# A two-layer attention and MLP kernel: one write and one read for each LayerNorm tile that is transposed through DRAM, Q and K weights loaded by halves, and a new written-out order

## The chip, the cores and the metric

The kernel runs on one core of a Trainium2 chip. A core has TensorE (PE, matrix multiplication), VectorE (DVE), ScalarE (ACT), GpSimd (POOL) and SyncE (SP), which here only issues DMAs, and 16 DMA engines that move data between the on-chip memory and DRAM. The metric is the device time of one execution in microseconds (us), lower is better. Three timed executions of the kernel before took 459.1, 463.7 and 463.11 us, so the median is 463.11 us.

## What is computed

The input x has 2048 rows of 512 features, in bf16. Two layers follow each other, each an attention and an MLP, with the same weights both times:

```python
x = x + attention(layernorm(x))
x = x + mlp(layernorm(x))
x = x + attention(layernorm(x))
x = x + mlp(layernorm(x))

# attention: 32 heads of 16, a query sees its own key and the 255 before it
qkv = x @ wqkv                                  # 512 -> 3 * 512
p = softmax(where(mask, q @ k.T * 16 ** -0.5, -1e9))
return (p @ v) @ wo
# mlp
return gelu(x @ w1 + b1) @ w2 + b2              # 512 -> 1792 -> 512
# layernorm
(x - mean) / sqrt(var + 1e-5)
```

## The kernel before

**Tiles.** The 2048 rows are 16 tiles of 128 rows; since there are two layers, the code counts 32 tiles `tau`, 0 to 31, where tile 16 is tile 0 in the second layer. Attention goes in 16 blocks `b` of two tiles. For each block the code makes Q (`lnq`), K and V (`kv`), then in `attention` the scores (`visit`: matmuls of 32 by 64, and an exponential on ScalarE, L938), the mask (L959, on VectorE or POOL), the product with V (`pv`), the output projection and the residual sum into X (`outproj`, `residual`). The MLP runs in ten jobs `J` of two or four tiles (`mlp`): W1, gelu on ScalarE, W2, residual sum. A block of attention needs the Q of the next block too, as a key is seen by the 255 queries behind it.

**LayerNorm and the transposition.** `layernorm(tau, layer, ...)` (L726) serves both: `layer` 0 is the one ahead of attention, `layer` 1 the one ahead of the MLP. Statistics are taken on VectorE (L733, L735), eps is added on VectorE (L737), POOL takes the power -0.5 (L740), and VectorE scales the tile into `xn` (L743). A matmul wants the features on the partitions, so the tile must be transposed. It goes one of two ways. Early tiles, and the last two ahead of the MLP, go through TensorE (L769 to L778) and are copied to `xnTA` (attention) or `xnTB` (MLP). The others, for which `by_dma` is true (tiles 4 to 29 ahead of the MLP, 14 to 31 ahead of attention, 44 in all), go through DRAM: VectorE transposes blocks of 32 by 32 into `xs_` (L752), four DMAs of 32 partitions each write `xs_` to a scratch tensor in DRAM (L764), and one DMA reads it back in the transposed layout (L767). Ahead of attention the four writes are cut into runs of 64 bytes (2048 in a tile), ahead of the MLP into runs of 256 bytes (512 in a tile); the read is 128 rows of 1 KB in both. All five are issued by SP, in its order, and the read waits for all four writes.

**The loads.** `load` and `load_x` (L689, L694) issue the inputs at the start. SP's queue has X 0, X 2-3, X 4-7, b1, Wo, X 8-15, W1, W2, b2; ScalarE's queue has X 1 and then Wqkv in three parts of 512 columns: Q, K, V (L701 to L704). Here X n is tile n of x.

**What sets the order.** Every operation is added to a list by `add()` with its engine, the names that it reads and writes, and a duration that a planner once used. Some operations have an alternative engine (`alt`). Three tables are written out by hand: `ORDER`, the sequence in which the operations are issued (each engine runs its own in that sequence), `TURNS`, which of the alternatives is taken, and `BANKS`, which banks of PSUM each matmul group gets. `_List.run` goes through them and `_Sched.op` adds the semaphore waits. DMAs take 12 semaphores in turn, and a DMA waits for the one 12 places ahead of it. An engine never passes over a waiting instruction, so where an operation stands in `ORDER` decides what waits behind it. A read of a name waits for its last write: the names `Wqkv0`, `Wqkv1` and `Wqkv2` are the three parts of Wqkv, `xa..` the tiles of `xnTA`, `xb..` those of `xnTB`, `scr..` the places in DRAM.

## Time and profile before

| | before |
|---|---|
| timed executions | 459.1, 463.7, 463.11 us (median 463.11) |
| profiled execution | 460.17 us, its span 458.4 us, mean granted clock 0.996 |
| matmuls | 8690 records, 427.1 us busy |
| DMA | 22.88 MB, 68606 packets, 54188 of them under 512 bytes |
| issues of `xs_` to DRAM | 176, each 32 KB |
| reads back | 26 into `xnTB`, 18 into `xnTA`, each 128 KB |

How to read it: the span is the stretch of the profiled execution in which the core's engines worked; the execution's own time is 1.8 us more. "Busy" is the time in which an engine had an instruction in work, and "idle before" a group of instructions is put down to what released it: `<-DMA xnTB<-scr_x` is a wait for the transfer from the scratch tensor to `xnTB`. "SPq" and "ACTq" are the instruction queues of SP and ScalarE that issue DMAs. "PEld" is TensorE's weight load, beside the matmuls. The granted clock is the share of TensorE's full clock that it was given. A window's row has its start and end, its length, then for each engine busy us and (x instructions).

### The profile page before, as it was taken

How to read it: one execution, taken by the hardware profiler on the slowest of the kernel's cores; microseconds unless marked ns; L12 is line 12 of the kernel's file. 1: busy time of each engine (PE TensorE's matmuls, PEld its weight loads, DVE VectorE, ACT ScalarE, POOL GpSimd, SP SyncE). 2: the span in 40 equal slices, each digit the busy share in tenths (PEclk: the TensorE clock that was granted, in tenths of full speed). 3: DMA queues.
4: the chain of work that ended last, by engine and by line, in shares of the span. 5: the costliest groups of instructions: out<-in, count | busy, mean ns of one | idle time of the engine just before them, and what ended most of it. 6: DMA issues, size and time to landing. Idle time of an engine off the chain costs nothing.

```text
span 458.4 us, 19424 instructions
## 1 busy us (share of the span) xinstructions
PE 427.1 (93%) x8690; PEld 232.9 (51%) x8764; DVE 370.1 (81%) x753; ACT 388.6 (85%) x463; POOL 232.3 (51%) x266
## 2 busy tenths in 40 slices
PE   5998999988999999699999999999998899999997
PEld 2655564655444555354444535445463453445665
DVE  4899988899998999678998789999796868576432
ACT  2699999999999989689998999989998799884343
POOL 4277555564764645643657557364444532554120
PEclk9899999999999999999999999999999999999999
DMA  8910000001230232301132112302223012102011
GB/s 280 370 53 3 4 3 3 3 4 28 42 68 14 30 64 43 69 10 37 27 72 46 20 34 50 72 17 31 47 57 69 4 36 48 49 4 70 13 47 57
DMA packets 68606, 22.88 MB, mean 50 GB/s; under 512 B 54188, under 2 KB 68012, under 8 KB 68524
## 3 DMA queue, kind: packets, MB, share of 16 engines
q1 hardware_dynamic: 66796, 19.94, 19.7%
q10 hardware_dynamic: 1728, 1.70, 1.1%
q8 instruction: 68, 1.11, 1.0%
q14 instruction: 14, 0.11, 0.1%
HBM read 13.77 MB, written 7.86 MB: 47 GB/s over the span
## 4 chain that ended last, share of the span: by engine, by line
PE 60%; ACT 17%; DMA 8%; DVE 8%; SPq 4%; issue 3%; ACTq 0%; DVEq 0%
PE ps L32 59%; ACT E L938 12%; DMA scr_x<-xs_ 3%; SPq L764 3%; DMA xnTB<-scr_x 3%; ACT gT L1104 2%; DMA Wqkv_sb<-in_A_wqkv_dram 2%; DVE X L796 1%; ACT gT L1096 1%; DVE xs_ L752 1%; DVE E L959 1%; DVE stat L733 1%; DVE TT L1024 1%; DVE KT L859 1%; DVE QT L719 1%
## 5 line engine op out<-in xcount | busy, mean ns | idle before, releaser
L938 ACT ACTIVATE E<-ps 128x1024 bf16<-128x1024 f32 x304 | 286.4, 1046 | 27.1 <-PE ps L32 26.0
L959 POOL TENSOR_TENSOR E<-E,mask 128x512 bf16<-128x512 bf16 (+1 forms) x131 | 135.3, 1047 | 108.6 <-ACT E L938 41.4
L32 PE MATMUL ps<-xnTB,W_sb 128*128 128x512 bf16 (+1 forms) x560 | 115.6, 337 | 5.3 <-DMA xnTB<-scr_x 4.6
L32 PE MATMUL ps<-W_sb,gT 128*128 128x512 bf16 (+1 forms) x421 | 108.5, 373 | 5.4 <-issue 3.5
L32 PE MATMUL ps<-xnTA,Wqkv_sb 128*128 128x256 bf16 (+1 forms) x544 | 74.4, 271 | 5.5 <-DMA Wqkv_sb<-in_A_wqkv_dram 3.1
L32 PEld LDWEIGHTS ps<-xnTB,W_sb 128*128 128x128 bf16 x560 | 51.0, 98 | 50.1 <-DMA xnTB<-scr_x 4.9
L1104 ACT ACTIVATE gT<-ps,b1T 128x512 bf16<-128x512 f32 (+1 forms) x92 | 49.0, 590 | 23.8 <-PE ps L32 23.7
L32 PE MATMUL ps<-QT,KT 32*64 32x320 bf16 (+4 forms) x2976 | 65.2, 258 | 2.8 <-ACT E L938 2.0
L796 DVE TENSOR_TENSOR X<-X,ps 128x512 bf16<-128x512 bf16 x63 | 42.5, 679 | 27.4 <-PE ps L32 27.3
L32 PEld LDWEIGHTS ps<-W_sb,gT 128*128 128x128 bf16 x462 | 41.4, 98 | 42.7 <-issue 5.6
L32 PEld LDWEIGHTS ps<-xnTA,Wqkv_sb 128*128 128x128 bf16 x544 | 48.0, 100 | 27.2 <-ACT E L938 4.3
L740 POOL TENSOR_TENSOR rstd<-veps,mhalf 128x1 f32<-128x1 f32 x64 | 37.2, 588 | 40.1 <-DVE veps L737 39.5
L959 DVE TENSOR_TENSOR E<-E,mask 128x512 bf16<-128x512 bf16 (+1 forms) x131 | 49.5, 403 | 6.3 <-ACT E L938 6.3
L32 PEld LDWEIGHTS ps<-QT,KT 32*64 32x64 bf16 x2976 | 27.5, 103 | 49.9 <-ACT E L938 32.9
L1068 POOL TENSOR_TENSOR X<-X,b2b 128x512 bf16<-128x512 bf16 x32 | 36.8, 1156 | 31.5 <-DVE TM L1029 15.1
L1024 DVE STREAM_TRANSPOSE TT<-ps 128x1024 f32<-128x1024 f32 x32 | 39.9, 1248 | 13.4 <-PE ps L32 13.1
L32 PE MATMUL ps<-E,Va 64*17 64x128 bf16 (+3 forms) x3872 | 46.1, 229 | 4.5 <-issue 0.9
L32 PEld LDWEIGHTS ps<-E,Va 64*17 64x17 bf16 x3872 | 36.8, 85 | 20.0 <-PE ps L32 7.2
L733 DVE BATCH_NORM_STATS2 stat<-X 128x6 f32<-128x512 bf16 x64 | 43.4, 681 | 2.8 <-DMA X<-in_A_x_dram 2.1
L1093 DVE TENSOR_SCALAR gT<-ps,b1T 128x512 bf16<-128x512 f32 (+1 forms) x48 | 31.7, 671 | 12.2 <-PE ps L32 11.6
L859 DVE TENSOR_TENSOR KT<-ps,parmask 128x1024 bf16<-128x1024 f32 x30 | 36.2, 1213 | 4.9 <-PE ps L32 4.7
L1029 POOL TENSOR_TENSOR TM<-TT,Rc 128x512 bf16<-128x512 f32 x21 | 22.3, 1061 | 28.8 <-DVE Rc L1027 19.7
(51 smaller groups left out, 333.7 us busy)
## 6 DMA issues: line engine op xcount, KB each, us to landing
scr_x<-xs_ SPq DMA_DIRECT2D x176, 32.0 KB, 2.2
W_sb<-in_B_w_dram SPq DMA_DIRECT2D x2, 1792.0 KB, 17.8
xnTB<-scr_x SPq DMA_DIRECT2D x26, 128.0 KB, 2.3
xnTA<-scr_x SPq DMA_DIRECT2D x18, 128.0 KB, 2.4
out_dram<-X SPq DMA_DIRECT2D x15, 128.0 KB, 1.8
Wqkv_sb<-in_A_wqkv_dram ACTq DMA_DIRECT2D x3, 512.0 KB, 9.3
X<-in_A_x_dram SPq DMA_DIRECT2D x1, 1024.0 KB, 13.0
X<-in_A_x_dram SPq DMA_DIRECT2D x1, 512.0 KB, 7.7
```

What stands on the lines that cost most here:

```text
L32: return self.e.matmul(*a, **k)
L733: add("dve", lambda e, B: e.bn_stats(stat6[:, k6, :], X[:, t, :]), 590, reads=["X%d" % t], writes=["st%d" % k6], prio=prio)
L740: add("pool", lambda e, B: e.tensor_tensor(out=rstd[:, k : k + 1], in0=veps[:, k : k + 1], in1=mhalf[:], op=ALU.pow), 535, reads=["ve%d" % ...
L796: add("dve", lambda e, B: e.tensor_tensor(out=X[:, t, :], in0=X[:, t, :], in1=ps[:, B[g][0], :], op=ALU.add), d_psum(512), reads=["X%d" % ...
L859: add("dve", lambda e, B, g=g, i=i: e.tensor_tensor(out=KT[:, kb, :, 2 * i : 2 * i + 2, :].rearrange("p a c q -> p a (c q)"), in0=ps[:, B[ ...
L938: add("act", lambda e, B, g_=g_, gi=gi: e.activation(E[:, 2 * gi : 2 * gi + 2, e0 : e0 + 512], ps[:, B[g_][0] : B[g_][0] + 2, :], AF.Exp, ...
L959: op = lambda e, B, Ew=Ew, Mw=Mw: e.tensor_tensor(out=Ew, in0=Ew, in1=Mw, op=ALU.mult)
L1024: add("dve", lambda e, B: e.transpose(TT[:, s].rearrange("p a c q d -> p a (c q d)"), ps[:, B[g][0] : B[g][0] + 2, :].rearrange("p a n -> ...
L1029: mul = lambda e, B: e.tensor_tensor(out=TM[:, sm].rearrange("p c q a d -> p a (c q) d"), in0=TT[:, s, :, :, :, 0:Dh].rearrange("p a c q d ...
L1068: add("pool", lambda e, B: e.tensor_tensor(out=X[:, t, :], in0=X[:, t, :], in1=b2b[:], op=ALU.add), 1110, reads=["X%d" % t, "b2b"], writes ...
L1093: add("dve", lambda e, B, g=g, fc=fc: e.tensor_scalar(out=gT[:, fc, 0:M], in0=ps[:, B[g][0], 0:M], scalar1=b1T[:, fc : fc + 1], scalar2=No ...
L1104: add("act", lambda e, B, g=g, fc=fc: e.activation(gT[:, fc, 0:M], ps[:, B[g][0], 0:M], AF.Gelu_apprx_tanh, bias=b1T[:, fc : fc + 1], scal ...
```

## The change

Four things change.

1. The transposition through DRAM has one write in place of four. To allow it the features are permuted in one way for both layers (`(d j q)` where the MLP's had `(d q j)`), and the pieces of the layout that the four writes made are now made by the read. Ahead of the MLP the write is 128 rows of 1 KB and the read 512 runs of 256 bytes; ahead of attention the write is 512 runs of 256 bytes and the read 2048 runs of 64 bytes. The planned durations are new, with 0.7 us added from tile 12 on (`room`).
2. The columns of Q and of K in Wqkv are loaded as halves of 256 columns, in the order Q first half, K first half, Q second, K second, then V whole. They stand on SP's queue behind X 0. X 2-3 goes to ScalarE's queue behind X 1. The projections wait for the half that they use.
3. The addition of eps may run on POOL instead of VectorE.
4. `ORDER`, `TURNS` and `BANKS` are new throughout.

```diff
-        load_x(0, 1, 2600.0)
-        load_x(1, 1, 2700.0, "act")
-        for which, lands in enumerate((5000.0, 7000.0, 9800.0)):
-            load(lambda e, B, which=which: e.dma_start(
-                Wqkv_sb[:, :, which * D : (which + 1) * D],
-                A_wqkv[:, which * D : (which + 1) * D].rearrange("(c p) n -> p c n", p=P)), ["Wqkv%d" % which], lands, "act")
-        load_x(2, 2, 4700.0)
-        load_x(4, 4, 9000.0)
...
+        def load_w(lo, n, name, lands):
+            load(lambda e, B: e.dma_start(
+                Wqkv_sb[:, :, lo : lo + n], A_wqkv[:, lo : lo + n].rearrange("(c p) n -> p c n", p=P)), [name], lands)
+
+        load_x(0, 1, 2450.0)
+        load_x(1, 1, 2650.0, "act")
+        load_x(2, 2, 4500.0, "act")
+        for i, lands in enumerate((4600.0, 5500.0, 6300.0, 7200.0)):
+            load_w(i % 2 * D + i // 2 * D // 2, D // 2, "Wqkv%d_%d" % (i % 2, i // 2), lands)
+        load_w(2 * D, D, "Wqkv2", 9000.0)
+        load_x(4, 4, 10700.0)
...
-            add("dve", lambda e, B: e.tensor_scalar(
-                out=veps[:, k : k + 1], in0=statmv[:, k, 1:2], scalar1=EPS, scalar2=None, op0=ALU.add), 75,
-                reads=["mv%d" % k], writes=["ve%d" % k], prio=prio - 300)
+            eps = lambda e, B: e.tensor_scalar(
+                out=veps[:, k : k + 1], in0=statmv[:, k, 1:2], scalar1=EPS, scalar2=None, op0=ALU.add)
+            add("dve", eps, 75, reads=["mv%d" % k], writes=["ve%d" % k], prio=prio - 300, alt=(("pool", eps, 130),))
...
+                order_ = "p (q d j) -> p d q j" if layer else "p (d q j) -> p d q j"
                 add("dve", lambda e, B: e.transpose(
-                    xs_[:, z, :].rearrange("p (q d j) -> p d q j", q=4, d=DC), 
-                    xn[:, s, :].rearrange("p (d q j) -> p d q j" if layer else "p (d j q) -> p d q j", q=4, d=DC)), 630,
+                    xs_[:, z, :].rearrange(order_, q=4, d=DC), xn[:, s, :].rearrange("p (d j q) -> p d q j", q=4, d=DC)), 630,
                     reads=["xn%d" % s], writes=["xs%d" % z], prio=prio)
                 flat = scr[v].rearrange("p c -> (p c)")
-                for r in range(4):
-                    if layer:
-                        to = scr[v].rearrange("(q j) (r c) -> r j q c", j=32, r=4)[r]
-                        src = xs_[32 * r : 32 * r + 32, z, :].rearrange("j (q c) -> j q c", q=4)
-                    else:
-                        to = flat.rearrange("(j x r k) -> r j x k", j=32, r=4, k=32)[r]
-                        src = xs_[32 * r : 32 * r + 32, z, :].rearrange("j (x k) -> j x k", k=32)
-                    dma(lambda e, B, to=to, src=src: e.dma_start(to, src), ["scr%d_%d" % (v, r)], reads=["xs%d" % z],
-                        prio=prio, dur=2000.0 if layer else 3000.0, issue=400.0)
-                to = dst.rearrange("p r d j -> p (r d j)") if layer else xnTA[:, tau // 2 % 2, tau % 2].rearrange("p c t -> p (c t)")
-                dma(lambda e, B, to=to: e.dma_start(to, scr[v]), [dname], reads=["scr%d_%d" % (v, r) for r in range(4)], prio=prio, dur=2300.0, issue=420.0)
+                if layer:
+                    put = lambda e, B: e.dma_start(scr[v], xs_[:, z, :])
+                    get = lambda e, B: e.dma_start(
+                        dst.rearrange("p r d j -> p r (d j)"), flat.rearrange("(r p c) -> p r c", r=4, p=P))
+                else:
+                    put = lambda e, B: e.dma_start(
+                        flat.rearrange("(d p c) -> p d c", d=DC, p=P), xs_[:, z, :].rearrange("p (d c) -> p d c", d=DC))
+                    get = lambda e, B: e.dma_start(
+                        xnTA[:, tau // 2 % 2, tau % 2].rearrange("p d (r k) -> p (d r) k", r=4),
+                        flat.rearrange("(x p k) -> p x k", x=16, p=P))
+                room = 0.0 if tau < 12 else 700.0
+                dma(put, ["scr%d_0" % v], reads=["xs%d" % z], prio=prio, dur=(2200.0 if layer else 2500.0) + room, issue=440.0 if layer else 600.0)
+                dma(get, [dname], reads=["scr%d_0" % v], prio=prio, dur=(2700.0 if layer else 3600.0) + room, issue=600.0 if layer else 1100.0)
                 return
...
-                         P, DC, ["xa0_%d" % j, "Wqkv%d" % which], prio, fresh=(j == 0))
+                         P, DC, ["xa0_%d" % j, "Wqkv%d_%d" % (which, kc // 2)], prio, fresh=(j == 0))
...
-                         256, 2, xr + ["Wqkv%d" % which], prio, fresh=(half == 0), war=war)
+                         256, 2, xr + ["Wqkv%d_%d" % (which, i)], prio, fresh=(half == 0), war=war)
```

## The prediction

> **What bounds the kernel now.** I read the page's busy times first, then the waits of TensorE, then its busy time by windows, and last the chain and the timeline of the two places where TensorE stands still.

> ```profile
> span 458.4 us, 19424 instructions
> PE 427.1 (93%) x8690; PEld 232.9 (51%) x8764; DVE 370.1 (81%) x753; ACT 388.6 (85%) x463; POOL 232.3 (51%) x266
> ```

> ```profile
> PE ps L32 <- issue: 7.2, 40, 0.9
> PE ps L32 <- DMA xnTB<-scr_x: 5.7, 4, 3.3
> PE ps L32 <- ACT E L938: 4.8, 17, 0.5
> PE ps L32 <- DMA Wqkv_sb<-in_A_wqkv_dram: 3.1, 2, 2.0
> ```

> ```profile
> 0.00:5.00 5.00, 3.76 (x9) 1.34 (x10) 1.92 (x6) 1.28 (x1) 3.66 (x17) 1.00 0.60 187
> 5.00:11.00 6.00, 2.68 (x25) 1.57 (x23) 3.40 (x13) 1.19 (x2) 1.75 (x3) 1.00 1.08 352
> 11.00:15.00 4.00, 3.93 (x44) 3.75 (x45) 2.14 (x4) 1.53 (x4) 0.00 (x0) 0.65 1.10 360
> ...
> 20.00:30.00 10.00, 9.87 (x175) 5.63 (x183) 9.76 (x24) 10.00 (x13) 7.75 (x8) 1.00 0.50 160
> ...
> 190.00:200.00 10.00, 8.44 (x200) 4.65 (x201) 5.46 (x12) 6.11 (x7) 4.17 (x7) 1.00 0.41 71
> ...
> 340.00:350.00 10.00, 8.42 (x244) 4.20 (x253) 7.04 (x13) 8.03 (x9) 7.51 (x7) 1.00 0.37 56
> ```

> The second fence is us in total, times, longest. The columns of the third are PE, PEld, DVE, ACT and POOL busy, granted clock, DMA share, GB/s. TensorE works 427.1 of 458.4 us, so all its idle time is 31.3 us, and nothing in the change removes a matmul. What can be won is idle time: 5.7 us in four waits for the transposed rows of the MLP (`xnTB`), 3.1 us in two waits for Wqkv, and what hangs on them. After the start ScalarE is full (10.00 of 10 in 20 to 30 us), so there the time is set by when its exponentials begin. Around 190 and 340 us all engines sag together (ACT 6.11 and 8.03): a transfer is the bound there.

> **The start.** The rows are those of the timeline.

> ```profile
> 3.24 1.09 SPq L695 DMA_DIRECT2D X<-in_A_x_dram  x1
> 6.49 1.23 ACT L721 ACTIVATE xnTA<-ps 128x512 bf16<-128x512 bf16 x2 [2.37 <-PE ps L36]
> 8.24 1.43 SPq L711 DMA_DIRECT2D W_sb<-in_B_w_dram  x1
> 8.46 0.41 DVE L743 TENSOR_SCALAR xn<-X,statmv,rstd 128x512 bf16<-128x512 bf16 x1 [0.37 <-POOL rstd L740]
> 11.07 1.07 PE L32 MATMUL ps<-xnTA,Wqkv_sb 128*128 128x128 bf16 x16 [2.01 <-DMA Wqkv_sb<-in_A_wqkv_dram]
> 12.62 0.63 PE L36 MATMUL ps<-ident,xn 128*128 128x128 bf16 x4
> 13.05 3.16 PE L32 MATMUL ps<-xnTA,Wqkv_sb 128*128 128x128 bf16 x24
> 13.29 0.42 DVE L719 COPY xnTA<-ps 128x512 bf16<-128x512 bf16 x1 [0.88 <-PE ps L36]
> 16.03 0.60 ACT L721 ACTIVATE QT<-ps 128x512 bf16<-128x512 f32 x1 [1.49 <-PE ps L32]
> 17.17 5.61 ACT L938 ACTIVATE E<-ps 128x1024 bf16<-128x1024 f32 x6 [0.55 <-PE ps L32]
> 17.26 0.60 PE L32 MATMUL ps<-xnTA,Wqkv_sb 128*128 128x256 bf16 x4
> ```

> The fourth normalized tile is ready at 8.46 + 0.41 = 8.87, but TensorE stands in its order before the K weights until 11.07, and that tile is transposed only at 12.62. The first exponential needs the Q of the second block, so those tiles, and starts at 17.17.

> With the change X 0, then half of Q, half of K, the other halves and V come on SP's queue, X 1 and X 2-3 on ScalarE's. Bytes ahead of the first K half: 512 KB of X and 512 KB of weights at most, 1.05 MB. The core moved 187 GB/s x 5 us = 0.94 MB by 5.0 us and 352 GB/s after it: landed near 5.3 us; the second halves (1.57 MB) near 6.8, V (2.10 MB) near 8.3. Tile 0's transposed rows are there at 6.49 + about 0.6 = 7.1. So no weight is waited for and the 3.1 us go. What is late next is VectorE's LayerNorm chain. I numbered the add() calls to read the new list: VectorE does four statistics, four scales and one evacuation more (0.42) before the fourth tile is ready, about 9.3 us; then the transpose (0.63 at most), evacuation 0.42, eight matmuls of 256 columns (1.2 by the last row, 4 in 0.60), evacuation 0.60, scores about 0.5: the first exponential at 12.8 with no gaps, 13.9 with a tenth or so lost at each handover. That is 3.3 to 4.4 us earlier than 17.17. VectorE was 9.76 of 10 busy in 20 to 30 us and has now less done in advance, so some comes back: bounds 1.0 and 4.4, and I take 3.3, nearer the upper end, since ScalarE (10.00) and not VectorE was the fuller engine. X 4-7, moved behind the weights (2.6 MB, about 9.8 us), X 8-15, W1 and W2 come about 1 us later than now; VectorE turns to X 4-7 only past 12 us, so I cost that at nothing.

> The granted clock was 0.65 in 11 to 15 us, behind 6 us in which TensorE was busy for 2.68; the 24 matmuls at 13.05 ran under it. The eight matmuls of Q would take up to 1.2 us more if that came again. [...]

> **The transfers.** The chain that ended last, at the worst place:

> ```profile
> 178.31 0.71 DVE xs_ L752
> ...
> 182.58 1.44 SPq L764
> 184.06 0.56 SPq L764
> 184.66 4.04 DMA scr_x<-xs_
> 189.23 2.23 DMA xnTB<-scr_x
> 191.50 4.96 PE ps L32 x48
> ```

> ```profile
> L764 SPq DMA_DIRECT2D scr_x<-xs_ x176: 302/555/2017, 105.3 to 420.1; - x176
> L767 SPq DMA_DIRECT2D xnTB<-scr_x x26: 320/338/1406, 113.1 to 421.8; - x26
> L767 SPq DMA_DIRECT2D xnTA<-scr_x x18: 320/388/747, 135.5 to 351.7; - x18
> ```

> ```profile
> scr_x<-xs_ SPq DMA_DIRECT2D x176, 32.0 KB, 2.2
> xnTB<-scr_x SPq DMA_DIRECT2D x26, 128.0 KB, 2.3
> xnTA<-scr_x SPq DMA_DIRECT2D x18, 128.0 KB, 2.4
> out_dram<-X SPq DMA_DIRECT2D x15, 128.0 KB, 1.8
> ```

> ```profile
> SPq L767 <- DMA scr_x<-xs_: 27.1, 21, 3.4
> ```

> From the transpose at 178.31 to the matmul at 191.50 it is 13.2 us: SP issues the writes of two tiles and more one by one, the last write lands after 4.04, then the read. SP spends 176 x 0.555 = 97.7 us on writes, plus 16 on reads, and 27.1 us standing before reads whose writes haven't landed, with the next tile's writes queued behind it.

> A tile alone takes three issues ahead of the last (1.67), 2.2 to land, 2.3 or 2.4 for the read: 6.2 us. Now one write and one read. For the MLP (26 tiles) the write has the form of the output (128 rows of 1 KB, 1.8 us); the read is 512 runs of 256 bytes in place of 128 of 1 KB, at least the 2.3 of now. For attention (18 tiles) the write is 512 runs of 256 bytes, and the read 2048 runs of 64 bytes, which no row shows. The DMA part of two windows (100 to 120 and 140 to 170 us, in this order) bounds a short run by packets, MB and share of 16 engines' time:

> ```profile
> q1 hardware_dynamic: 1440, 0.52, 12.5%
> ...
> q1 hardware_dynamic: 7488, 0.85, 20.6%
> ```

> The first is mostly 256-byte writes: 0.125 x 16 x 20 us / 1440 = 28 ns each. The second is mostly 64-byte writes: 0.206 x 16 x 30 / 7488 = 13 ns. So the 128 runs that each of 16 engines reads cost 1.7 to 3.6 us in place of about 0.4 (128 KB at 352 GB/s), and the read lands in 2.4 to 5.5 us; the MLP's read (32 runs, 0.4 to 0.9) in 2.3 to 3.0. The trip is 4.1 to 4.8 us for an MLP tile (1.4 to 2.1 less) and 4.2 to 8.0 for an attention tile (from 2.1 less to 1.7 more). I take 4.4 and 6: the short-run write is the nearest row to a short-run read. SP's own time goes by the rows issued: 1.09 us for 1024 rows (X 8-15), 1.43 for 1792 (W2), so 0.8 to 0.95 an MLP tile and 2.0 to 2.5 an attention tile, where five issues took 2.6.

> [...]

> At 178.31 the new trip is two writes and two reads in SP's queue: about 5 to 8 us to the matmul where 13.2 were, so the 3.3 us wait goes. The other three share 2.4 us; the four together are 5.7. Bounds for this part, with 64-byte reads in their lower half: 2 and 5.7; I take 4.5, since the new list moves the places, and a last tile's read now may come close to its user (in the new list the first MLP group has less TensorE work between transpose and use than before).

> **The rest.** Of the 64 additions of eps 34 go to POOL (rows below: VectorE loses 34 x 0.142 = 4.8 us, POOL gains about as much).

> ```profile
> L737 DVE TENSOR_SCALAR veps<-statmv 128x1 f32<-128x1 f32 x64 | 8.7, 142 | 0.8
> ```

> Each may now queue behind a POOL mask of about 1 us ahead of the reciprocal root; and VectorE has 9.76 of 10 busy only early (5.46 and 7.04 in the two late windows above). Bounds -1 and +1, taken as 0. Table loads (18) and switches of TensorE's array shape (362 against 360) stay by the lists; 128 masks in place of 131 run on POOL.

> **Sum.** 3.3 + 4.5 = 7.8 us. The profiled execution took 460.17 us around its span of 458.4; against it the sum gives 452.4. The median of the three timed runs (459.1, 463.7, 463.11) is 463.1, 2.9 higher, and gives 455.3. I say 455.

> **The rivals.**

> First, the late attention reads, which end slower. If a 64-byte read costs like 28 ns or more, two tiles of a block keep the 16 engines for 7.2 us, the second lands up to 1.7 + 3.6 = 5.3 us later than now, and MLP reads queue behind it. QKV of the next block then waits in nine blocks. It decides from 0.9 us a block (9 x 0.9 is the whole gain); with 2 us a block, 18 - 7.8 = 10 us slower, 473. For it: no row has such reads. Against: TensorE has no wait for `xnTA` of a transfer now, so there is some slack, and the 64-byte writes go at 13 ns.

> Second, the waits for `xnTB` come back at other places, as the new list puts users closer behind the reads: only the start's 3.3 us stay, 459.8. For it: all four groups of an MLP job wait for the last of four tiles. Against: SP's queue is half empty.

> Third, the start is given back because VectorE (9.76 of 10) can't feed ScalarE: 1.0 + 4.5 gives 457.6.

> **How the numbers follow.** The forecast has 0.64, the late reads 0.14, returning waits 0.12, the lost start 0.10. About 1% is what a measurement of this kernel can tell from no change. Faster by over 1% (under 458.5): 0.60 + 0.03 + 0.03 = 0.66. Slower by over 1%: 0.13 of the first rival. The rest, 0.21, is within 1%. The low end takes both upper bounds, 4.4 + 5.7 + 1, off the profiled run: about 449; and the spread of the runs, 448.5. The high end takes in the second and third rivals and a third of the first: 462.5. The forecast's own range is 449 to 458.

> **What would show it.** Right: the first exponential starts at 12.8 to 14 us, no wait of TensorE for Wqkv; the waits for `xnTB` fall from 5.7 to near 1; MLP reads land in 2.3 to 3.0 us, attention reads in 2.4 to 5.5, SP issues for 57 to 70 us in place of 114. Wrong: attention reads over 6 us, a new line of TensorE waiting for `xnTA`, ScalarE with gaps in 13 to 30 us, or a half clock there.

## The result, and the profile after

The change made the kernel slower, by 0.8%. The median of 20 timed executions is 459.79 us (458.15 to 465.06), that of the kernel before, 20 executions beside them, 457.52 us (452.99 to 463.7). The ratio of after to before is 1.0078, 95% interval 1.0051 to 1.0105. The profiled execution took 463.4 us with a span of 461.5; in the profiled one of before these were 460.17 and 458.4.

The page of after, its waits of TensorE (us in total, times, longest), and its windows (columns as in the prediction):

```profile
span 461.5 us, 19292 instructions
PE 438.4 (95%) x8764; PEld 233.9 (51%) x8764; DVE 369.4 (80%) x723; ACT 387.4 (84%) x462; POOL 239.4 (52%) x297
```

```profile
PE ps L36 <- DVE xn L740: 6.5, 1, 6.5
PE ps L32 <- issue: 3.9, 5, 2.1
PE ps L32 <- ACT E L937: 3.5, 12, 0.7
```

```profile
5.00:11.00 6.00, 1.14 (x5) 0.35 (x3) 0.00 (x0) 1.28 (x1) 0.00 (x0) 0.80 1.01 319
11.00:15.00 4.00, 1.66 (x15) 1.40 (x16) 3.67 (x11) 0.60 (x1) 1.68 (x4) 0.50 1.11 353
15.00:20.00 5.00, 5.00 (x52) 4.91 (x51) 3.63 (x8) 0.87 (x2) 1.42 (x3) 0.62 1.03 395
...
140.00:150.00 10.00, 9.41 (x159) 4.36 (x166) 6.36 (x10) 7.12 (x8) 6.62 (x7) 0.83 0.02 3
190.00:200.00 10.00, 10.00 (x265) 5.63 (x264) 9.90 (x20) 8.48 (x11) 5.41 (x9) 1.00 0.44 69
340.00:350.00 10.00, 10.00 (x246) 5.82 (x244) 9.36 (x14) 8.23 (x11) 4.71 (x5) 1.00 0.34 82
```

Both waits that the change was to remove are gone: TensorE has no line for `xnTB` (5.7 us before) and none for Wqkv (3.1). The windows around 190 and 340 us, where TensorE had 8.44 and 8.42 of 10, are full. But one wait of 6.5 us is new, from 5 to 11 us VectorE does nothing at all, and two stretches have a lower granted clock: 5 to 20 us (0.80, 0.50, 0.62) and 140 to 150 us (0.83). TensorE's busy time, 438.4 us, can't be set against the 427.1 of before: that trace lacks the records of 74 matmuls (8690 beside 8764 weight loads), this one lacks none.

The timeline of after at the start:

```profile
0.79 0.38 SPq L689 DMA_DIRECT2D X<-in_A_x_dram  x1
1.22 2.61 SPq L694 DMA_DIRECT2D Wqkv_sb<-in_A_wqkv_dram  x5
4.39 1.35 ACTq L689 DMA_DIRECT2D X<-in_A_x_dram  x2
11.18 0.69 DVE L730 BATCH_NORM_STATS2 stat<-X 128x6 f32<-128x512 bf16 x1 [7.42 <-DMA X<-in_A_x_dram]
12.65 0.61 PE L36 MATMUL ps<-ident,xn 128*128 128x128 bf16 x4 [6.51 <-DVE xn L740]
21.23 1.03 ACT L937 ACTIVATE E<-ps 128x1024 bf16<-128x1024 f32 x1
```

ScalarE's queue issues X 1 only at 4.39 us and X 2-3 behind it, although nothing stands ahead of them on that queue. By then the weights and X 4-7 are under way, so X 1 lands at 11.15, VectorE waits 7.42 us for it, and the first exponential starts at 21.23; before it was 17.17.

Where the time came and went, worked out from the trace: ScalarE's 304 exponentials come in one order in every version, so the start of the k-th, less its start in the kernel before, is a running account (us; E1, E5, E6 and E12 are experiments below):

```
exponential  before   after      E1     E5     E6    E12
  1           17.2     +4.1    -4.2   -4.1   -4.4   -4.0
 61           81.6     +4.0    -4.1   -4.2   -4.5   -4.0
101          126.7     +4.7    -2.9   -3.6   -3.9   -2.9
111          136.9     +7.7    -0.3   -4.2   -2.7   -1.6
141          177.8     +9.6    +1.4   -2.9   -1.2   -0.2
151          193.8     +5.7    -2.3   -6.9   -1.2   -4.1
261          347.3     +6.1    -1.5   -7.0   -1.5   -4.4
271          361.3     +2.9    -4.8  -10.2   -4.7   -7.6
304          407.4     +2.8    -4.9  -10.3   -4.8   -7.8
```

In after, 4.1 us are lost at the start, 3.0 between the 101st and the 111th, and 1.9 more by the 141st. Then 3.9 come back at the 151st and 3.2 at the 271st. The small steps between add 0.9, and the sum is +2.8.

The table shows where time goes better than how much, for two reasons. It compares single executions: those of before and after took 2.7 and 3.6 us more than the medians of their kernels, that of E5 2.1 less (by the medians after is at +2.3, E1 at -4.0, E5 at -6.0, E6 at -3.3, E12 at -4.9). And the new order moves TensorE's other work against the exponentials. Counted by the weight loads so far, each at its matmul's mean time, TensorE has done 1.0 us more at the 141st exponential than in before, 0.4 more at the 151st, 0.5 more at the 261st and 0.4 less at the 271st. So 1.0 of the 1.9 us is work moved forward, and the two gains are nearer 3.3 and 2.3 us (estimates from the trace).

The loss near the 101st is a stall in which TensorE waits for nothing that was released (timeline of TensorE in after), followed by matmuls that take up to twice as long (two of 512 columns 1.06 us at 142.89, where two took 0.60 at 136.62; the granted clock was 0.50 from 141.71 to 145.12):

```profile
137.16 1.34 PE L32 MATMUL ps<-E,Va 64*17 64x64 bf16 x94
140.59 0.56 PE L32 MATMUL ps<-E,Va 64*17 64x256 bf16 x38 [2.09 <-issue]
141.08 0.42 PE L32 MATMUL ps<-QT,KT 32*64 32x320 bf16 x16
141.43 1.66 PE L32 MATMUL ps<-Wqkv_sb,xnTA 128*128 128x512 bf16 x4
142.89 1.06 PE L32 MATMUL ps<-xnTB,W_sb 128*128 128x512 bf16 x2
```

The DMA queues of after (packets, MB, share of 16 engines), first from 134 to 137.5 us, then from 137.5 to 140.6:

```profile
q1 hardware_dynamic: 3692, 0.34, 75.5%
```

```profile
q1 hardware_dynamic: 1014, 0.06, 22.4%
q8 instruction: 1, 0.02, 3.0%
```

Queue 8 is of the kind "instruction" on the page, with 68 packets of 16 KB, and they go with TensorE's progress: 8764 weight loads and as many matmuls make 258 instructions for each. I read a packet as a block of about 256 of TensorE's instructions, a code block (an estimate from these counts). In the kernel before, the one that belongs here starts when TensorE has issued about 5285 instructions (weight loads and matmuls counted in the trace); in after it starts at 5468, behind 3692 packets in 3.5 us, of which 3098 are 64-byte reads of the first two attention tiles. The stall ends 1.4 us after it has landed. That was a reading of the trace only; E3, E5, E7 and E12 test it.

The issues and their transfers in after (median us to landing, then issue times min/median/max in ns, then SP's waits):

```profile
scr_x<-xs_ SPq DMA_DIRECT2D x44, 128.0 KB, 2.0
...
xnTB<-scr_x SPq DMA_DIRECT2D x26, 128.0 KB, 2.7
xnTA<-scr_x SPq DMA_DIRECT2D x18, 128.0 KB, 3.7
```

```profile
L755 SPq DMA_DIRECT2D scr_x<-xs_ x26: 319/332/1291, 114.3 to 421.2; - x26
L756 SPq DMA_DIRECT2D xnTB<-scr_x x26: 359/371/1512, 117.4 to 423.4; - x26
L759 SPq DMA_DIRECT2D scr_x<-xs_ x18: 359/360/1013, 131.1 to 356.0; - x18
L761 SPq DMA_DIRECT2D xnTA<-scr_x x18: 359/360/1356, 134.4 to 360.1; - x18
```

```profile
SPq L756 <- DMA scr_x<-xs_: 16.0, 14, 2.1
...
SPq L761 <- DMA scr_x<-xs_: 11.8, 7, 3.4
```

SP stands in front of reads as long as before (27.8 against 27.1 us), but behind it far less is queued, so nobody waits for it.

### The profile page after: what moved, and what is told of

It is laid out like the page before. It is cut to its first block, busy times and chain, and to the rows that moved or that the text cites. A ratio compares the mean times of both kernels' runs of the same rounds, so it can differ in the third digit from the quotient of the medians.

```text
span 461.5 us, 19292 instructions
## 1 busy us (share of the span) xinstructions
PE 438.4 (95%) x8764; PEld 233.9 (51%) x8764; DVE 369.4 (80%) x723; ACT 387.4 (84%) x462; POOL 239.4 (52%) x297
## 4 chain that ended last, share of the span: by engine, by line
PE 77%; ACT 14%; DVE 3%; DMA 3%; issue 1%; SPq 0%
PE ps L32 77%; ACT E L937 12%; DMA X<-in_A_x_dram 1%; DMA scr_x<-xs_ 1%; DVE KT L858 1%; DMA Wqkv_sb<-in_A_wqkv_dram 1%; ACT gT L1103 1%; PE ps L36 1%; DVE stat L730 0%; DVE xs_ L750 0%; DVE X L795 0%; ACT gT L1095 0%; ACT L937 0%; ACT L1103 0%; DVE TT L1023 0%
## 5 line engine op out<-in xcount | busy, mean ns | idle before, releaser
L32 PE MATMUL ps<-W_sb,gT 128*128 128x512 bf16 (+1 forms) x462 | 119.8, 374 | 0.9 <-issue 0.6
L32 PE MATMUL ps<-xnTB,W_sb 128*128 128x512 bf16 (+1 forms) x560 | 116.5, 339 | 1.1 <-ACT E L937 0.5
L32 PE MATMUL ps<-xnTA,Wqkv_sb 128*128 128x256 bf16 (+1 forms) x544 | 75.6, 273 | 2.0 <-ACT E L937 1.2
L32 PEld LDWEIGHTS ps<-xnTB,W_sb 128*128 128x128 bf16 x560 | 51.3, 98 | 46.0 <-ACT E L937 5.1
L32 PE MATMUL ps<-QT,KT 32*64 32x320 bf16 (+4 forms) x2976 | 65.5, 259 | 2.8 <-ACT E L937 1.2
L32 PEld LDWEIGHTS ps<-W_sb,gT 128*128 128x128 bf16 x462 | 41.0, 98 | 44.5 <-issue 8.1
L32 PEld LDWEIGHTS ps<-xnTA,Wqkv_sb 128*128 128x128 bf16 x544 | 48.9, 101 | 24.5 <-ACT E L937 4.3
L958 DVE TENSOR_TENSOR E<-E,mask 128x512 bf16<-128x512 bf16 (+1 forms) x134 | 52.8, 421 | 3.6 <-ACT E L937 3.3
L32 PEld LDWEIGHTS ps<-QT,KT 32*64 32x64 bf16 x2976 | 27.8, 103 | 49.5 <-ACT E L937 32.5
L32 PE MATMUL ps<-E,Va 64*17 64x128 bf16 (+3 forms) x3872 | 46.5, 229 | 5.5 <-issue 3.0
L1023 DVE STREAM_TRANSPOSE TT<-ps 128x1024 f32<-128x1024 f32 x32 | 39.9, 1247 | 13.1 <-PE ps L32 12.8
L737 POOL TENSOR_TENSOR rstd<-veps,mhalf 128x1 f32<-128x1 f32 x64 | 37.2, 586 | 24.3 <-DVE veps L734 22.5
L32 PEld LDWEIGHTS ps<-E,Va 64*17 64x17 bf16 x3872 | 36.7, 85 | 22.5 <-PE ps L32 8.2
L32 PE MATMUL ps<-Wqkv_sb,xnTA 128*128 128x512 bf16 x128 | 37.6, 386 | 0.4 <-issue 0.3
## 6 DMA issues: line engine op xcount, KB each, us to landing
scr_x<-xs_ SPq DMA_DIRECT2D x44, 128.0 KB, 2.0
xnTB<-scr_x SPq DMA_DIRECT2D x26, 128.0 KB, 2.7
xnTA<-scr_x SPq DMA_DIRECT2D x18, 128.0 KB, 3.7
out_dram<-X SPq DMA_DIRECT2D x15, 128.0 KB, 1.8
```

Of the source, the lines that this page charges most:

```text
L32: return self.e.matmul(*a, **k)
L737: add("pool", lambda e, B: e.tensor_tensor(out=rstd[:, k : k + 1], in0=veps[:, k : k + 1], in1=mhalf[:], op=ALU.pow), 535, reads=["ve%d" % ...
L958: op = lambda e, B, Ew=Ew, Mw=Mw: e.tensor_tensor(out=Ew, in0=Ew, in1=Mw, op=ALU.mult)
L1023: add("dve", lambda e, B: e.transpose(TT[:, s].rearrange("p a c q d -> p a (c q d)"), ps[:, B[g][0] : B[g][0] + 2, :].rearrange("p a n -> ...
```

## The experiments

The theory for the start: DMAs take 12 semaphores in turn. Counted in the new `ORDER`, all 13 loads of SP's queue are issued ahead of X 1 and X 2-3, which makes these the 14th and 15th DMA; the 14th must wait until the second, the first half of Q, has landed, and the 15th for the third, the first half of K. In the trace of after these two land at 4.37 and 5.25 us, and X 1 and X 2-3 are issued at 4.39 and 5.27. The rival: X 1 is late because SP's queue crowds it out, whenever it is issued. The theory for 132 to 141 us: TensorE's code block is held up by the 64-byte reads; rivals are the reads themselves coming late for their users, or the new order.

Each kernel was timed beside the kernel before on its chip: E1 to E4 together (median before 459.17 us, 35 executions), E5 to E8 (458.29, 25), E9 to E11 (457.96, 23), E12 (458.33, 15).

### E1: X 1 and X 2-3 issued right behind X 0

```diff
+        ORDER = [i for i in ORDER if i not in (19, 20)]
+        ORDER[ORDER.index(18) + 1 : ORDER.index(18) + 1] = [19, 20]
```

> The changed kernel, with the issue of X 1 and X 2-3 moved up in the written order to right behind X 0 (nothing else). In the changed kernel X 1 is the 14th DMA of the list, so with 12 semaphores in turn it waits for the second one, the first half of Q, and is issued at 4.39 us. Theory (semaphore turn): X 1 is issued at 0.8 us and lands near 3.3, the first exponential starts at 13 to 14 us in place of 21.2, and all that follows comes 7 to 8 us earlier: span 453 to 455, about 1.1% under the kernel before. Rival (crowding): X 1 is late because SP's queue holds the 16 DMA engines with 2 MB of weights; then X 1 still lands past 7 us, and the gain over the changed kernel is under 3 us. The stall of TensorE near 138 us stays by either, some 7 us earlier.

Measured: 455.19 us, ratio 0.992 (0.9888 to 0.9952), span 453.8. The timeline of E1:

```profile
0.79 0.91 ACTq L691 DMA_DIRECT2D X<-in_A_x_dram  x2
...
4.18 0.66 DVE L732 BATCH_NORM_STATS2 stat<-X 128x6 f32<-128x512 bf16 x1
...
12.97 3.78 ACT L939 ACTIVATE E<-ps 128x1024 bf16<-128x1024 f32 x4
```

The first exponential starts 8.3 us earlier than in after, and two list entries account for more than the whole loss. The bytes on SP's queue are the same, so crowding is not the cause. What stays is the stall: 1.87 us at 132.77, and in the table 2.6 us lost between the 101st and the 111th exponential.

### E2: 16 semaphores in place of 12

```diff
-N_DMA_SEMS = 12
+N_DMA_SEMS = 16
```

> The changed kernel in its own order, with 16 DMA semaphores in turn in place of 12, so that the 14th and 15th DMA have fresh ones. Theory (semaphore turn): as with the loads moved up, X 1 is issued near 0.8 us and the first exponential starts at 13 to 14 us; span 453 to 455. Rival (crowding): X 1 is issued early but lands past 7 us, and the span is above 458.

Measured: 454.61 us, ratio 0.9905 (0.9873 to 0.9938); X 1 is issued at 0.79 and the first exponential starts at 12.95, with the order as changed. So it is the reuse of the semaphore that held X 1 back. E1 and E2 cannot be told apart in time.

### E3: attention tiles read back in rows of 1 KB

```diff
-                        xnTA[:, tau // 2 % 2, tau % 2].rearrange("p d (r k) -> p (d r) k", r=4),
-                        flat.rearrange("(x p k) -> p x k", x=16, p=P))
+                        xnTA[:, tau // 2 % 2, tau % 2].rearrange("p d t -> p (d t)"), scr[v])
```

This brings the same bytes in 128 runs of 1 KB, so the features of those tiles reach the matmuls in the wrong places (in E5 too); the work is the same.

> The changed kernel, with the attention tiles read back as 128 rows of 1 KB in place of 2048 runs of 64 bytes. The features land in the wrong places, so the attention is computed on mixed-up features; all times but that of this read are as they were. Theory (code behind short runs): TensorE's stall of 2.1 us at 138.5 comes from its next instructions, which are fetched by the same DMA engines and stood behind 3500 packets of 64 bytes; with wide reads the fetch starts some 1.5 us earlier, the stall and the half clock after it go, and the time falls by 2.5 to 3.5 us (span 458 to 459); reads land in 2.4 in place of 3.7 us. Rival (order): the stall belongs to the new order of TensorE's instructions and stays, the change in time is under 1 us.

Measured: 459.94 us, ratio 1.0032 (0.9996 to 1.0068), span 457.8 against 461.5 of after. The windows of E3:

```profile
130.00:140.00 10.00, 8.70 (x256) 4.13 (x254) 7.60 (x14) 8.59 (x10) 6.14 (x7) 1.00 0.30 68
140.00:150.00 10.00, 9.84 (x140) 4.64 (x126) 9.04 (x15) 9.72 (x11) 7.42 (x7) 1.00 0.01 3
```

The clock dip behind 140 us is gone (0.83 to 1.00), the stall there is 1.10 us in place of 2.09, the code block starts at instruction 5324, and the exponentials lose 0.7 us in place of 3.0 between the 101st and the 111th. So about 2.3 us come from the 64-byte reads, a little less than the 2.5 to 3.5 expected, and as half of the stall stays, they are not its only cause. The ratios differ by 0.46%, 2.1 us, and their intervals just overlap; the trace, not the time, carries this one.

### E4: the loads as before, with the rest of the change

X 0, X 2-3, X 4-7 on SP's queue, X 1 and Wqkv in three whole parts on ScalarE's; everything else as changed.

> The changed kernel with the loads of the kernel before: Wqkv in three whole parts on ScalarE's queue behind X 1, X 2-3 on SP's. By the traces the changed kernel loses 4.0 us before the first exponential and 3.1 between the 100th and the 110th, and wins 4.0 near 190 us and 3.3 near 350. Theory: without the late X 1 the first exponential is back at 17 to 18 us and the transfers' part of the change stands alone: 3.5 to 4 us faster than the changed kernel, span 457 to 458, level with the kernel before or up to 1% faster. If the halves on SP's queue are worth what was forecast (3.3 us), the kernel with X 1 moved up is 3 to 4 us faster than this one. Rival: the late start costs nothing by the end, since ScalarE catches up, and the time stays within 1 us of the changed kernel.

Measured: 457.91 us, ratio 0.9998 (0.996 to 1.0036), first exponential at 15.89, one wait of 3.0 us for Wqkv. The change without its new start is level with the kernel before: what the saved transfers bring is spent elsewhere. E1 less E4 is the worth of the new loads when they are issued at once: 0.8% by the ratios (3.6 us), 2.7 us by the medians, 1.4 us by the last exponentials of the two traces.

### E5: E1 and E3 together

> X 1 moved up and the attention tiles read back as 128 rows of 1 KB (features mixed up, so the attention is computed on wrong features; all else as it was). With X 1 moved up alone the time is 0.992 of the kernel before, and TensorE still stands 1.87 us at 132 us for its code, with a half clock after it. Theory (code behind short runs): that goes too, 2 to 3 us more, span 450.5 to 452, ratio 0.985 to 0.988: with both faults away the change gives about the 7.8 us forecast. Rival: the two overlap, the stall's time is won back later anyway, and the ratio stays above 0.989.

Measured: 452.26 us, ratio 0.9901 (0.9862 to 0.994), span 448.4, clock 1.000 throughout. The windows and the waits of TensorE in E5:

```profile
130.00:140.00 10.00, 9.84 (x185) 4.84 (x169) 8.48 (x14) 9.65 (x11) 7.97 (x8) 1.00 0.01 3
```

```profile
PE ps L32 <- issue: 8.0, 44, 0.5
```

With both faults out, no stall is longer than 0.53 us and nothing is lost between the 101st and 111th exponential. (In the 8.0 us, 39 of the 44 waits are gaps of 0.16 us. The trace of after, which lacks no record, has none of these; here 77 records of matmuls are missing.) By medians it is 6.0 us below the kernel before. The ratio misses the 0.985 to 0.988 that was expected, though its interval reaches them.

### E6: E1 with attention tiles written by four transfers, as before

Attention tiles again take four writes in 64-byte runs and one read in rows of 1 KB; MLP tiles as changed.

> X 1 moved up, the MLP tiles with one write and one read, the attention tiles the way of the kernel before (four writes of 64-byte runs, one read of 128 rows). The output is the reference's. Theory (it is reads of short runs that hold the code fetch, as the kernel before wrote the same runs without such a stall): no stall near 131 us, ratio 0.985 to 0.990. Rival (short runs in either direction hold it): the stall stays near 2 us and the ratio is 0.991 or more. SP has three more issues for each attention tile, so waits of TensorE for transfers may come back: if over 3 us of them do, the ratio is above 0.992 as well and the profile tells which.

Measured: 454.98 us, ratio 0.9947 (0.9916 to 0.9979). The waits of TensorE in E6:

```profile
PE ps L32 <- issue: 8.0, 44, 0.5
...
PE ps L32 <- DMA xnTB<-scr_x: 3.9, 3, 2.2
```

The stall is gone (the code block starts at instruction 5276, although 2616 writes of 64 bytes went in the 4 us before it, where E1 had 3455 reads), but three waits for `xnTB` are back: 72 writes of attention tiles stand in SP's queue ahead of the MLP's. In the table E6 gains 2.4 us over E1 up to the 111th exponential, loses them at the 151st, and ends where E1 does. One write for the attention tiles is worth about what its 64-byte read costs. So the 0.985 to 0.990 of the theory was missed, by the waits that the expectation had named as the exception.

### E7: E1 with 42 more instructions of TensorE ahead of everything

```diff
-        for n, took in ((8, 3420.0), (5, 1500.0)):
-            add("pe", clear(n), took,
+        for work, took in ((clear(8), 3420.0), (small(26), 1500.0)):
+            add("pe", work, took,
```

`small(26)` makes 26 matmuls of 64 columns where `clear(5)` made 5 of 512. That puts every later instruction 42 places further on against the code blocks.

> X 1 moved up, and the second group of 5 zero matmuls that warm TensorE at the start replaced by 26 tiny ones (16 columns of weights, 64 of data): 42 more instructions ahead of all others, so TensorE's code blocks of 256 instructions end 42 instructions earlier in its work. The fetch that came due when the 64-byte reads had begun (instruction 5285 against 5283) then comes due about 0.7 us before them. Theory (code behind short runs): that fetch starts before the reads, the stall of 1.87 us and the half clock go with the 64-byte reads unchanged, span 450.5 to 452, ratio 0.985 to 0.989. Rival (the stall belongs to the data or the place in the work): it stays at the same matmul and the ratio is 0.991 or more.

Measured: 465.52 us, ratio 1.0196 (1.0146 to 1.0246). The stall at 132 us is gone, as expected, but nine others of 0.75 us or more have come, 11.6 us in all, and the time is far from the 0.985 to 0.989 expected. The waits, and the first, seventh and ninth of those stalls in the timeline of E7:

```profile
PE ps L32 <- issue: 18.4, 51, 1.9
```

```profile
46.76 0.36 PE L32 MATMUL ps<-QT,KT 32*64 32x192 bf16 x2 [1.55 <-issue]
...
265.33 0.22 PE L32 MATMUL ps<-E,Va 64*17 64x64 bf16 x8 [1.63 <-issue]
...
297.29 0.27 PE L32 MATMUL ps<-QT,KT 32*64 32x192 bf16 x3 [1.95 <-issue]
```

At 46.76 us no tile goes through DRAM yet. So a code block can come late without any 64-byte read: where its boundary falls in the program is enough. The theory that only the reads matter fell here.

### E8: E1 with all additions of eps on VectorE

> X 1 moved up, and all 64 additions of eps on VectorE, as in the kernel before, at their places in the new order. The prediction took their move at 0, with bounds of 1 us either way. Theory: ratio within 0.25% of that with X 1 moved up alone (0.992). Rival (the move to POOL is a part of the gain or the loss): 0.989 or less, or 0.995 or more.

Measured: 457.07 us, ratio 1.0 (0.9962 to 1.0038) against 0.992 of E1. One window of E1 and of E8:

```profile
20.00:30.00 10.00, 9.32 (x217) 5.55 (x210) 9.61 (x23) 10.00 (x12) 7.09 (x8) 1.00 0.58 184
```

```profile
20.00:30.00 10.00, 9.41 (x169) 5.79 (x174) 9.99 (x23) 9.06 (x12) 6.79 (x8) 1.00 0.57 181
```

The rival holds. Ahead of 20 us VectorE has six additions where E1 has two, and the first exponential comes at 13.51 us in place of 12.97. From 20 to 30 us, with work left over, VectorE is full (9.99) and ScalarE no longer is (9.06 against 10.00). Moving 34 additions to POOL is worth 2.1 us by the last exponential of the two traces, 1.9 by the medians and 0.8% by the ratios.

### E9 and E10: E1 with 10 and with 20 more instructions of TensorE

```diff
-        for n, took in ((8, 3420.0), (5, 1500.0)):
+        for work, took in ((clear(8), 3420.0), (warm(), 1500.0)):
```

`warm()` is `clear(5)` and then 5 (E9) or 10 (E10) matmuls of 64 columns.

> X 1 and X 2-3 right behind X 0, and five tiny matmuls more in the second warm-up, which moves every later instruction of TensorE on by 10 places against the blocks of 256 in which its code arrives. Theory (the block due at about instruction 5285 comes late because 64-byte reads start just before it): with 10 places the request may fall ahead of part of the reads; the stall of 1.9 us at 132 us shrinks below 1 us, the other stalls stay under 1 us, median 451 to 454 us, ratio 0.984 to 0.991. Rival (another boundary falls badly, as with 42 places): stalls at other places sum to over 4 us and the ratio is 0.995 or more.

> As the run before it, with ten tiny matmuls more, 20 places. Theory: the request of the block falls clear of the reads, the stall at 132 us is gone, median 450.5 to 453 us, ratio 0.983 to 0.989. Rival (another boundary falls badly, as with 42 places): stalls at other places sum to over 4 us and the ratio is 0.995 or more.

Measured: E9 458.88 us, ratio 1.0009 (0.9975 to 1.0042); E10 462.04 us, ratio 1.007 (1.0031 to 1.0108). The rival holds. The stall at 132 us stays in both (1.81 and 1.88 us; the block starts at instructions 5454 and 5461, still behind the reads), and others come: 5.4 us in E9, 5.6 in E10. E10 has two more, of 1.63 us at 204.12 and 2.09 at 266.85, which the profile puts down to VectorE; but that release came 0.25 and 0.33 us earlier, and both end 1.4 us after a code block has landed, as the others do. One of E9 in the timeline:

```profile
177.48 0.29 PE L32 MATMUL ps<-QT,KT 32*64 32x320 bf16 x1 [1.44 <-issue]
```

### E11: the kernel before with 42 more instructions of TensorE

`warm()` as in E10, with 21 small matmuls, in the kernel before.

> The kernel before with 21 tiny matmuls more in its second warm-up, 42 places, and nothing else. Theory (the place of the block boundaries matters to every version of this kernel): stalls of TensorE with nothing released sum to over 6 us where the kernel before has one of 0.95 us, and the ratio is 1.01 to 1.025. Rival (only the new order is fragile): stalls under 2 us, ratio within 0.998 to 1.005.

Measured: 472.12 us (4 executions), ratio 1.0314 (1.024 to 1.0387). Nine stalls of 0.88 us or more, 11.5 us in all, where the kernel before has one of 0.95. The ratio is above the 1.01 to 1.025 expected. So not only the new order is fragile. As it stands, the kernel before has its boundaries in mostly harmless places.

In the traces of before, after, E1, E7, E9, E10 and E11 there are 37 stalls of 0.45 us or more with nothing released. I counted the instruction (twice the number of weight loads so far) at which each ends, and the time since the last code block landed. Nine of the 37, worked out from the traces:

```
kernel  at us   stall  instruction  block landed before, us
E7      46.76   1.55    1714        1.43
E7     112.53   1.33    4514        1.37
E1     132.77   1.87    5528        1.43
E9     134.07   1.81    5528        1.24
after  140.59   2.09    5530        1.36
E9     177.48   1.44    7314        1.58
E10    179.62   1.60    7316        1.51
E7     265.33   1.63   10638        1.39
before 357.61   0.95   14464        1.40
```

To within 11, the instructions lie whole multiples of 255 apart (4514 - 1714 = 2800, eleven times less 5; 14464 - 1714 = 12750, fifty times), and they stay where they are when the program is moved by 10 or 20 places. All 37 stalls end 1.2 to 1.7 us after a block landed. So each is a wait for code at a block boundary. What the shift changes is which instructions stand in the block before the boundary: 128 matmuls of the product with V and their 128 weight loads, a whole block, take 1.64 us (timeline of E12 at 119.89), less than a block takes to come: its transfer lasts 0.9 to 1.9 us, and TensorE goes on 1.2 to 1.7 us after it has landed. In E7 and E11 the 128 matmuls ahead of each of the 18 stalls took 1.7 to 3.0 us; ahead of the other boundaries, as far as the count places them, about 7 us in the middle. A short block does not always stall: E7 has two of 2.1 us with no stall over 0.3.

### E12: E1 with only the first two attention tiles in the old form

Tiles 14 and 15 ahead of attention are written by four transfers and read in rows of 1 KB; the other 16 as changed. No instruction of TensorE is added or moved.

```diff
+                early = not layer and tau in (14, 15)
+                order_ = "p (q d j) -> p d q j" if layer or early else "p (d q j) -> p d q j"
...
+                elif early:
+                    for r in range(4):
+                        to = flat.rearrange("(j x r k) -> r j x k", j=32, r=4, k=32)[r]
+                        src = xs_[32 * r : 32 * r + 32, z, :].rearrange("j (x k) -> j x k", k=32)
+                        dma(lambda e, B, to=to, src=src: e.dma_start(to, src), ["scr%d_%d" % (v, r)], reads=["xs%d" % z],
+                            prio=prio, dur=3000.0, issue=400.0)
```

> X 1 and X 2-3 right behind X 0, and only the first two attention tiles of the DMA way (14 and 15) written by four transfers and read back in rows of 1 KB, all others as changed. No instruction of TensorE is added or moved. Theory (the stall at 132 us comes from these two tiles' 64-byte reads alone): the stall of 1.87 us and the half clock behind it are gone, one wait for xnTB of 1.0 to 1.6 us may stand near 128 us because SP has six writes more to issue there, the remaining attention tiles keep their saved waits, median 451.5 to 454 us, ratio 0.986 to 0.991. Rival (the eight writes cost SP as much as the reads cost TensorE): waits of TensorE for xnTB or xnTA of 2 us and more, ratio 0.992 or higher.

Measured: 453.47 us, ratio 0.9907 (0.9873 to 0.9941), span 451.2. The page (clock in 40 slices, 9 is full), the waits, and the timeline where TensorE now waits:

```profile
PEclk9999999999999999999999999999999999999999
```

```profile
PE ps L32 <- issue: 8.0, 45, 0.5
...
PE ps L32 <- DMA xnTB<-scr_x: 1.2, 1, 1.2
```

```profile
119.89 1.64 PE L32 MATMUL ps<-E,Va 64*17 64x64 bf16 x128
...
129.07 1.47 PE L32 MATMUL ps<-xnTB,W_sb 128*128 128x512 bf16 x6 [1.22 <-DMA xnTB<-scr_x]
```

The theory holds for the stall: it goes when these two tiles' reads go, the code block starts at 5276, and one wait of 1.2 us for `xnTB` is the price of six more writes on SP. That the half clock goes with them isn't shown: E2, E9 and E10 have the stall and no half clock behind it, and four of the ten executions of E12 have a granted clock of 0.995 or 0.996. In the running account E12 ends 2.9 us ahead of E1, by the medians 0.9. By the timed runs its interval overlaps those of E1 and E2, so which of the three is best isn't settled; each beats both kernels.

## Why the prediction was wrong, step by step

**What can be judged.** The 455 us were reckoned down from 463.1, the median of the first three executions of the kernel before. Twenty have 457.52, so 455 as such would have been a gain of 0.6% only, and that E1 measured 455.19 is luck. The forecast to judge is the gain of 7.8 us. Its 31.3 us of idle time are too many as well, as missing records count as idle there; no term of the sum hangs on that.

**The start is the step that failed.** The prediction put X 1 and X 2-3 first on ScalarE's queue and let them arrive as early as before. It worked out when the weights would land and what VectorE would then do, but did not number the two loads among the DMAs: as 14th and 15th of 12 semaphores they waited until 4.39 and 5.27 us (E1, E2). Forecast -3.3 us; measured +4.1. Most of the rest of the step was sound: with the loads issued at once the first exponential starts at 12.97 (forecast 12.8 to 13.9), no weight is waited for, and E1 less E4 is 1.4 to 3.6 us for the 3.3. The weights landed later than worked out (in E1 the first half of K at 6.31 for 5.3, the second halves by 8.43 for 6.8, V at 9.93 for 8.3); nobody waited for them, since the fourth tile was normalized only at 9.70 (forecast 9.3). The rule about the wait of a DMA for the one 12 places ahead was in the text that describes the kernel; it was never applied.

**The half clock.** The prediction priced it at 1.2 us at most, had no term for it in its sum and named it among the signs of being wrong. In after it came for 10.24 us, from 8.59 to 18.83, around a wait of TensorE of 6.51 us (6.14 to 12.65), and all 20 executions of after have a granted clock of 0.993 or less. In E1, with TensorE busy for 4.57 of 6 us from 5 to 11, the clock stayed at 1.00. The dips last 3.41 us or, in after's start, three times that, and in the 3.41 us ahead of each dip TensorE was busy for 0.97 to 1.98 us (1.40 in the kernel before, 0.97 and 1.32 in after), so it had not stood idle throughout. I divided all traces into steps of that length, placed by the edges of the dips. After each of the eight steps with 1.4 us busy or less the clock was 0.50, after 3 of 18 with 1.5 to 2.0, and after none with more, but for one inside the long dip, which had 2.07 (12.00 to 15.41 us in after). So in these traces it went by how a stall of 2 us fell into the steps whether a half clock followed: after, E1 and E8 have both at 132 to 141 us, E2, E9 and E10 a stall there of 1.8 to 1.9 us alone.

**The transfers.** The mechanism and the size of the saved waits were right: all four went, 5.7 us, where I took 4.5. In the running account after gains some 3.3 and 2.3 us at the two places, once the work moved forward is taken off. The attention reads landed in 3.0 to 5.2 us, median 3.7 (forecast 2.4 to 5.5), the MLP's in 2.1 to 4.0, median 2.7 (forecast 2.3 to 3.0), and nobody waited for `xnTA`. SP's issues were overrated: 0.33 to 0.37 us by the medians whatever the number of runs, 41 us in all, where I said 57 to 70. (Before they were 126 us in all and not 114, since I had multiplied medians; and the two rows that I took give 0.5 to 0.7 us for the 640 rows of an MLP tile, not 0.8 to 0.95.) What the step left out is the price of the 64-byte reads to a third party: some 2.3 us by the running accounts of after and E3 and 2.9 between E1 and E12, part of it the half clock, and 2.1 and 0.6 us by the ratios of the timed runs, for a code block of TensorE that comes behind them. With it, and without the new start, the change is level with the kernel before (E4). The first rival looked at the same reads, but for their own users.

**The rest.** Taken at 0 with bounds of 1 us, it is a gain of 1.9 to 3.7 us (E8 against E1): VectorE has little room early, as its 9.76 of 10 in the quoted window could have told. It is in all the other kernels with the change, so without it after would probably have been slower still; that was not run.

**The three rivals.** Nobody waited for the late attention reads, no wait for `xnTB` came back in after, and the start was not given back by VectorE: ScalarE has 9.91 of 10 in 20 to 30 us of after. Of the prediction's signs of being wrong two came: the half clock, and ScalarE with gaps in 13 to 30 us (its first exponential starts at 21.23). The slower side came by a mechanism that none of the rivals named.

**What stays open.** Between the 111th and the 141st exponential the five kernels of the table with the new order lose 1.3 to 1.9 us against before. About 1.0 us of it is work of TensorE moved forward; the cause of the rest I did not find. Nor is the forecast of 7.8 us confirmed: E5, with both faults out, gains 6.0 us by the medians, and as some 2 of them are the additions of eps, the start and the transfers together bring about 4 there (an estimate from E5, E1 and E8).

## What to carry to other kernels

Before pricing a load, number it among all the DMAs that share semaphores, across queues: in after X 1 is the first transfer of ScalarE's queue, and with 12 semaphores it was issued at 4.39 us, with 16 at 0.79 (E2). When a transfer is cut into thousands of short runs, ask what else uses the same DMA engines at that moment, the engines' own instructions among it: in after a code block came behind 3692 packets in 3.5 us, and TensorE stood still for 2.09. And when a kernel of many short matmuls is tuned, the place of its code blocks is part of the tuning: here 42 TensorE instructions more near the front shifted all of them, and cost 2.8% by the ratios in E7 (against E1) and 3.1% in E11.

## What the runs showed of the hardware

**Behind some 3500 short reads a code block came late, behind some 2600 short writes it did not.** With some 3500 reads of 64 bytes in the 4 us ahead of it the block started some 170 to 190 instructions of TensorE late (5452 in E1, 5468 in after, for 5285 in before); with some 2600 writes of 64 bytes it started at its usual place (5276 in E6 and in E12). The two differ in number too, so that a write is milder for itself isn't shown.

**A read of 2048 runs was issued as fast as one of 128:** 0.36 us in after, 0.39 in before (medians of 18), and it landed in 3.7 us where 128 runs landed in 2.4.

**A longer warm-up may have helped the start of the kernel before.** In E11 the warm-up of TensorE ended at 6.65 us in place of 6.24, the granted clock from 11 to 15 us was 1.00 in place of 0.65, and the first exponential came at 14.27 in place of 17.17. Part of it is that the K weights were waited for 0.7 us less in that execution. That the warm-up kept the clock up isn't shown: 36 of the 98 executions of the kernel before that were timed beside the experiments have a granted clock of 1.00 without it. The 2.9 us were lost again in the stalls.
